# Extra matmuls of the identity on TensorE in the first twelve pairs of an attention and feed-forward kernel

## The chip, the cores and the metric

The kernel runs on one core of a Trainium2 chip. A core has a matrix engine (TensorE, in the profile PE, with its weight loads as PEld), VectorE (DVE), ScalarE (ACT), GpSimd (POOL), and SyncE (SP), which here only issues DMAs. Each engine serves its own instructions in the order in which the program gives them, and engines wait for one another through semaphores. The metric is the time of one execution on the device in microseconds (us). The matrix engine accumulates in PSUM, which holds eight banks of 512 float32 columns on 128 partitions.

## The reference

```python
scores = (1 / sqrt(64)) * q @ k.T            # 8 batches, 12 heads, 448 x 64
m = max(scores, axis=-1)
e = exp(scores - m)
attn = e / (sum(e, axis=-1) + exp(-m) + 1e-09)
x = (attn @ v)                               # heads side by side: 3584 x 768
h = x @ w_in                                 # 768 x 2048
g = h * tanh(log(1 + exp(h)))
out = g @ w_out                              # 2048 x 768
```

All inputs and the output are float32; the kernel computes in bfloat16 with float32 accumulation.

## The kernel before

Work goes by pairs of heads: 48 pairs, six to a batch. A pair's scores are made in four steps. In pairs 0 to 11 each of the first three steps makes two blocks of 128 query rows, one of each head, from 64 rows of the transposed query and key (L255 and L258), and the fourth makes the two remaining blocks of 64 rows side by side (L263 and L266). From pair 12 on the two heads are laid out diagonally and one matmul of 128 rows makes both (L249).

PSUM is split into three score tiles of two banks each, taken in turn (`sc_tiles`), and two single banks (`mo_tiles`), which are handed out and given back through the deque `mo_free`. The fourth step of a pair uses only the first bank of its score tile.

A step runs so: `scores_ahead` lets TensorE write the scores of the step three ahead as soon as a score tile is free; VectorE reduces them to the negated row maximum (L270); `exps` lets ScalarE take the exponentials, which give the row sums too (L283), and that frees the tile. After a pair VectorE makes the denominators (L296, L300) and scales the exponentials (`normalise`, L317; in some pairs on GpSimd, L315). The result is turned by a transposing DMA (L321) or, for pairs 5, 6 and 7, by TensorE in `turn_on_pe` (L332, seven transposes into one single bank, copied out by VectorE, L336). `av_pair` multiplies with the values (L358), and the copy into `xT` (L367) follows in `flush_late`, which runs at the start of the next step. Queries and keys are loaded by SyncE (L121), cast on GpSimd (L162 to L164), transposed by TensorE (L179) and copied out (`evac_qk`).

The order of all this is written out by hand. The head of the program takes pairs 0 to 5, step by step. Then units of three pairs follow, twelve steps each; in the first two of them (pairs 6 to 8, and 9 to 11) the turns and the value products of earlier pairs are placed at given steps (`TURN_AT`, `AV_AT`). After the twelve steps of a unit TensorE makes eight column blocks of the first feed-forward product (`mm1_mish`, L382, with the Mish function on ScalarE, L388), between which the next pairs' transposes and first scores stand. From pair 12 on matmuls of the second feed-forward product (L446) are filled into the steps. Weights are loaded by GpSimd's queue in pieces at given steps (`load_w`, L148).

Of the kernel before, what the change touches and what calls it, by code (L numbers as in the profile page):

```python
# [19 lines left out]
def kernel(  # L20
# [9 lines left out]
    nc = tc.nc  # L30
# [18 lines left out]
    STEPS = 4  # L49
# [3 lines left out]
    def pool(name, bufs, space=None):  # L53
# [18 lines left out]
    sc_tiles = [  # L72
        psum.tile([128, 2, 512], FP32, tag=f"sc{i}", name=f"sc{i}") for i in range(3)
    ]
    mo_tiles = [psum.tile([128, 512], FP32, tag=f"mo{i}", name=f"mo{i}") for i in range(2)]
    mo_free = deque(mo_tiles)

    ident = singles.tile([128, 128], BF16)
# [24 lines left out]
    def flush_late():  # L103
        while late:
            late.popleft()()
# [8 lines left out]
    def load_pair(p):  # L114
        if p >= N_PAIRS:
            return
        b, h0 = p // HP, (p % HP) * 2
        tiles = []
        for nm, src in (("q", q), ("k", k), ("v", v)):
            t = ld_pool.tile([SP_, 2, NT * D], FP32, tag=f"{nm}_f", name=f"{nm}_f")  # L120
            nc.sync.dma_start(  # L121
                out=t, in_=src[b, h0 : h0 + 2].rearrange("h (p t) d -> p h (t d)", t=NT)
            )
            tiles.append(t)
        loaded[p] = tiles
# [19 lines left out]
    def load_w(n):  # L145
        for _ in range(min(n, len(pieces))):
            dst, src = pieces.popleft()
            nc.gpsimd.dma_start(out=dst, in_=src.rearrange("(a p) c -> p a c", p=128))  # L148
# [38 lines left out]
    def evac_qk(p, act=False):  # L187
        if p >= N_PAIRS:
            return
        (q_ps, k_ps), own = qkT[p]  # L190
        mo_free.extend(own)
        qd = q_diag[p % 3]
        kT = qk_pool.tile([128, S], BF16, tag="kT", name="kT")
        if p < DIAG_FROM:
            qT = qd.rearrange("d i h r -> d (i h r)")[:, 0:S]
            qkT[p] = (qT, kT)
            if act:
                nc.scalar.mul(qT, q_ps[:, 0:S], SCALE)
            else:
                nc.vector.tensor_scalar(  # L200
                    out=qT, in0=q_ps[:, 0:S], scalar1=SCALE, scalar2=None, op0=ALU.mult
                )
        else:
            qkT[p] = (qd, kT)
            if p < DIAG_FROM + 3:
                nc.vector.memset(qd[0:64, :, 1, :], 0.0)
                nc.vector.memset(qd[64:128, :, 0, :], 0.0)
            for h in range(2):
                rows = slice(64 * h, 64 * h + 64)
                nc.vector.tensor_scalar(  # L210
                    out=qd[rows, :, h, :],
                    in0=q_ps[rows, 0:S].rearrange("d (i r) -> d i r", i=QB),
                    scalar1=SCALE, scalar2=None, op0=ALU.mult,
                )
        if p == 0 or own and not act:
            nc.vector.tensor_copy(out=kT, in_=k_ps[:, 0:S])
        else:
            nc.scalar.copy(kT, k_ps[:, 0:S])  # L218

    rg = dict(next=0, used=0)  # L220

    def scores_ahead(limit):

        while rg["next"] < limit and rg["used"] < len(sc_tiles):
            rg["used"] += 1
            scores(rg["next"])
            rg["next"] += 1
# [67 lines left out]
    def denominators(st):  # L295
        nc.vector.scalar_tensor_tensor(  # L296
            out=st["den"], in0=st["sums"], scalar=1e-9, in1=st["expm"],
            op0=ALU.add, op1=ALU.add,
        )
        nc.vector.reciprocal(out=st["rden"], in_=st["den"])  # L300
# [158 lines left out]
    first_mm2 = 2 * UNITS_PER_B  # L459
# [23 lines left out]

    weight = [5.2] + [1.0] * (steps - STEPS) + [0.4] * (STEPS - 1)

    LEAD = UNIT_PAIRS + 1
    LOAD_AT = (0, 3, 6)
    HEAD = HP
# [9 lines left out]
    W_AT = ({5: 1, 9: 1}, {1: 1, 4: 1, 5: 1, 7: 1, 9: 1, 11: 1}, {3: 1, 5: 1, 7: 1, 9: 1})  # L498
    for p in range(UNIT_PAIRS):
        load_pair(p)  # L500
    for p in range(2):
        cast_pair(p)
        transpose_pair(p)
        if p == 0:
            evac_qk(p, act=True)
            scores_ahead(3)
    load_pair(3)
    cast_pair(2)


    for p in range(HEAD):
        for s in range(STEPS):
            if s == 1 and p == 0:
                transpose_pair(p + 2)
            exps(p * STEPS + s)
            if p == 0 and s == 0:
                evac_qk(1, act=True)
            if s == 1:
                evac_qk(p + 2, act=True)
            if s:  # L520
                flush_late()
            scores_ahead(HEAD * STEPS + 3)
            if s == (2 if p == HEAD - 1 else 0):
                load_pair(p + 4)
            if s == 0:
                cast_pair(p + 3)
                load_w(1)
                if p:
                    denominators(att[p - 1])
            if s == 1:  # L530
                if p:
                    normalise(p - 1)
            if s == 3 and p + 3 < HEAD + 2:
                transpose_pair(p + 3)
            if s == 3 and p >= 3:
                av_pair(p - 3, act=True)
# [3 lines left out]
    for u in range(UNITS_PER_B, N_UNITS + 2 * UNITS_PER_B):  # L540
        attn = u < N_UNITS
        filler = deque()
        for part in plan.get(u, []):
            filler.extend(mm2_part(*part))
        total, done, acc = sum(w for _, w in filler), 0, 0.0
        p0 = u * UNIT_PAIRS
        if attn and u >= first_mm2:
            av_with.update({p0 + i: p0 + i - UNIT_PAIRS for i in range(UNIT_PAIRS)})
        end = min((u + 1) * UNIT_PAIRS, N_PAIRS) * STEPS

        for n in range(steps):
            pi, s = divmod(n, STEPS)
            p, idx = p0 + pi, p0 * STEPS + n
            late_tp = u == UNITS_PER_B and n == STEPS
            if late_tp:
                transpose_pair(p0 + 2)
            exps(idx)
            if late_tp:
                evac_qk(p0 + 2)
            if u == UNITS_PER_B + 1:  # L560
                for part in TURN_AT[1].get(n, []):
                    turn_on_pe(*part)
            flush_late()
            acc += weight[n]
            want = int(total * acc / sum(weight) + 1e-6)
            while done < want:
                fn, w = filler.popleft()
                fn()
                done += w
            scores_ahead(end)  # L570
            if n in LOAD_AT:
                load_pair(p0 + LOAD_AT.index(n) + LEAD)
                cast_pair(p0 + LOAD_AT.index(n) + LEAD - 1)
            if u - UNITS_PER_B < len(AV_AT):
                early = AV_AT[u - UNITS_PER_B]
                if n in early:
                    av_pair(early[n])
                if u == UNITS_PER_B:
                    for part in TURN_AT[0].get(n, []):
                        turn_on_pe(*part)  # L580
            elif s == (2 if pi else 0) and N_PAIRS <= p < N_PAIRS + UNIT_PAIRS:
                av_pair(p - UNIT_PAIRS)
            if u - UNITS_PER_B < len(W_AT):
                load_w(W_AT[u - UNITS_PER_B].get(n, 0))
        assert done == total

        moe = u < N_UNITS + UNITS_PER_B
        b, w = (u - UNITS_PER_B) // UNITS_PER_B, u % UNITS_PER_B
        nxt = p0 + UNIT_PAIRS
        todo = sorted(range(p0, nxt), key=lambda p: p in BY_PE)  # L590
        for f in range(FF_U):
            if moe:
                mm1_mish(b, w * FF_U + f)
            if u == UNITS_PER_B and f in (2, 6):
                load_w(1)
            if not attn:
                continue
            if f == 0:
                denominators(att[p0]["whole"])
                normalise(todo[0], dma=todo[0] not in BY_PE)  # L600
            if f == 3:
                scores_ahead(min(nxt * STEPS + 1, N_PAIRS * STEPS))
            if f in (1, 3, 5):
                transpose_pair(nxt + f // 2, bank=f // 2 % 2)
                evac_qk(nxt + f // 2)
            if f >= FF_U - 2:
                scores_ahead(min(nxt * STEPS + f - FF_U + 4, N_PAIRS * STEPS))
            if f == 3:
                normalise(todo[1], dma=todo[1] not in BY_PE)
            if f == 4:  # L610
                normalise(todo[2], dma=todo[2] not in BY_PE, on_pool=True)
        if moe and w == UNITS_PER_B - 1:
            gather_mid(b)
# [32 lines left out]
```

## Time and profile before

| what | value |
|---|---|
| three runs | 487.44, 489.59, 489.74 us; median 489.59 |
| the profiled execution | 492.75 us, of which its span 491.0 |
| busy over the span: PE, DVE, ACT, POOL | 450.5, 351.3, 350.2, 161.5 us |
| PE busy in 12 to 24 us, and in 96 to 108 us | 6.57 and 11.92 of 12 us |
| score matmul of 64 rows and 448 columns (L255), median | 529 ns |
| score matmul of 128 rows and 448 columns (L249), median | 353 ns |

The span runs from the first to the last instruction of the program. A row of the timeline gives start, duration, engine, line, operation, the tile written and those read with their shapes, how many instructions are merged, and, in brackets, how long the engine had been idle and what ended the wait. The chain of waits follows the work that ended last back to the start. A window's row gives for each engine the busy time and the number of instructions in it, then the granted clock of TensorE, the share of the DMA engines and the data rate. Matmuls overlap in the pipeline, so seven of them last less than seven times one.

### The profile page before, as it was taken

The numbers are of one execution on the slowest core, as the hardware profiler recorded it, in microseconds if no ns is written. First come the engines' busy times: TensorE is split into PE (matmuls) and PEld (weight loads), VectorE is DVE, ScalarE is ACT, GpSimd is POOL, SyncE is SP. The second block draws the span as 40 slices with busy tenths as digits, with TensorE's granted clock in tenths as the row PEclk, the third lists the DMA queues.
The fourth block names the chain that finished last, engine by engine and source line by source line (L and its number), as shares of the span: only waits on it lengthen the run. The fifth ranks groups of instructions, "written<-read, shape, count | busy, mean of one in ns | idle before, by whom it ended". The sixth has DMA issues, their size and how long they took to land.

```text
span 491.0 us, 8804 instructions
## 1 busy us (share of the span) xinstructions
PE 450.5 (92%) x2992; PEld 248.5 (51%) x2992; DVE 351.3 (72%) x702; ACT 350.2 (71%) x906; POOL 161.5 (33%) x266
## 2 busy tenths in 40 slices
PE   3556898798989999999999999999999999999996
PEld 1222444454644555555655555555556565556563
DVE  4798987978868787878788786878797878420021
ACT  4889678878777887979796878888797979502300
POOL 3622257454412534253413323253425230300000
PEclk9999998999999999999999999999999999999999
DMA  8999999999999999999998979998999686780112
GB/s 212 183 205 228 236 207 221 228 177 236 175 225 263 195 220 188 241 186 267 148 248 187 223 164 210 211 213 227 176 265 179 167 176 140 132 159 21 45 37 93
DMA packets 209452, 92.19 MB, mean 188 GB/s; under 512 B 166272, under 2 KB 205952, under 8 KB 209408
## 3 DMA queue, kind: packets, MB, share of 16 engines
q1 hardware_dynamic: 201920, 85.35, 81.2%
q0 software_dynamic: 7488, 6.29, 8.8%
q8 instruction: 23, 0.38, 0.3%
q14 instruction: 21, 0.17, 0.1%
HBM read 45.61 MB, written 11.01 MB: 115 GB/s over the span
## 4 chain that ended last, share of the span: by engine, by line
PE 68%; DVE 14%; ACT 9%; DMA 4%; issue 2%; SPq 1%; POOL 0%; DVEq 0%; ACTq 0%
PE mo L446 24%; PE mo L382 23%; PE sc L249 8%; ACT en L283 8%; DVE negm L270 7%; PE sc L358 6%; DVE en L317 4%; PE sc L382 3%; PE sc L179 3%; DMA eT<-en 3%; DMA k_f<-in_k_dram 1%; PE mo L358 1%; PE sc L255 1%; DVE xT L367 1%; DVE eT L336 1%
## 5 line engine op out<-in xcount | busy, mean ns | idle before, releaser
L283 ACT ACTIVATE en<-sc,negm 128x448 bf16<-128x448 f32 x336 | 209.7, 637 | 28.7 <-DVE negm L270 16.3
L270 DVE TENSOR_REDUCE negm<-sc 128x2 f32<-128x896 f32 x192 | 182.4, 969 | 61.5 <-PE sc L249 48.7
L446 PE MATMUL mo<-w_out_sb,gT 128*128 128x384 bf16 (+1 forms) x896 | 142.1, 303 | 0.0
L382 PE MATMUL mo<-xT,w_in_sb 128*128 128x448 bf16 x672 | 140.2, 352 | 0.9 <-DVE xT L367 0.9
L388 ACT ACTIVATE gT<-mo 128x448 bf16<-128x448 f32 x112 | 59.4, 543 | 73.5 <-PE mo L382 73.3
L446 PEld LDWEIGHTS <-gT 128*128 128x128 bf16 x896 | 84.0, 98 | 46.8 <-issue 1.3
L382 PEld LDWEIGHTS <-w_in_sb 128*128 128x128 bf16 x768 | 72.8, 98 | 64.9 <-issue 4.2
L315 POOL TENSOR_SCALAR en<-en,rden 128x448 bf16<-128x448 bf16 x98 | 61.7, 649 | 115.8 <-DVE rden L308 106.0
L249 PE MATMUL sc<-kT,qd 128*128 128x448 bf16 x252 | 71.6, 354 | 1.8 <-DVE qd L210 1.5
L162 POOL CAST q_bf<-q_f 112x512 bf16<-112x512 f32 x47 | 29.1, 619 | 121.8 <-DMA q_f<-in_q_dram 105.4
L283 ACT ACTIVATION_READ_ACCUMULATOR en<-sc,negm 128x1 f32 x336 | 69.2, 206 | 0.0
L317 DVE TENSOR_SCALAR en<-en,rden 128x448 bf16<-128x448 bf16 x238 | 67.2, 354 | 0.9
L433 DVE COPY o_sb<-mo 128x384 f32<-128x384 f32 (+1 forms) x64 | 32.1, 502 | 41.3 <-PE mo L446 41.2
L249 PEld LDWEIGHTS <-qd 128*128 128x128 bf16 x252 | 24.0, 97 | 32.1 <-issue 13.9
L358 PE MATMUL sc<-eT,v_bf 112*64 112x448 bf16 x288 | 34.1, 357 | 4.1 <-ACT en L283 2.0
L164 POOL CAST v_bf<-v_f 112x512 bf16<-112x512 f32 x48 | 29.6, 618 | 20.6 <-DMA v_f<-in_v_dram 19.1
L358 PEld LDWEIGHTS <-v_bf 112*64 112x64 bf16 x384 | 21.1, 114 | 25.7 <-issue 16.9
L255 PE MATMUL sc<-kT,qd 64*128 64x448 bf16 x36 | 17.5, 508 | 17.4 <-ACT en L283 16.0
L163 POOL CAST k_bf<-k_f 112x512 bf16<-112x512 f32 x47 | 29.2, 622 | 6.7 <-DMA k_f<-in_k_dram 5.9
L210 DVE TENSOR_SCALAR qd<-sc 64x448 bf16<-64x448 bf16 x72 | 27.8, 386 | 0.9
L218 ACT COPY kT<-sc 128x448 bf16<-128x448 bf16 x39 | 20.8, 534 | 6.8 <-PE sc L179 6.8
L446 PE MATMUL mo<-w_out_sb,mid 128*128 128x384 bf16 x128 | 24.9, 326 | 0.0
(50 smaller groups left out, 306.9 us busy)
## 6 DMA issues: line engine op xcount, KB each, us to landing
q_f<-in_q_dram SPq DMA_DIRECT2D x48, 224.0 KB, 5.5
k_f<-in_k_dram SPq DMA_DIRECT2D x48, 224.0 KB, 5.6
v_f<-in_v_dram SPq DMA_DIRECT2D x48, 224.0 KB, 5.9
w_in_sb<-in_moe_w_in_dram POOLq DMA_DIRECT2D x12, 256.0 KB, 5.6
w_out_sb<-in_moe_w_out_dram POOLq DMA_DIRECT2D x8, 384.0 KB, 8.6
out_dram<-o_sb SPq DMA_DIRECT2D x7, 336.0 KB, 3.5
out_dram<-o_sb SPq DMA_DIRECT2D x8, 288.0 KB, 4.8
out_dram<-o_sb SPq DMA_DIRECT2D x8, 240.0 KB, 3.4
```

Of the source, the lines that this page charges most:

```text
L163: cast_k(out=k_bf, in_=k_f.rearrange(by_t, t=NT))
L164: nc.gpsimd.tensor_copy(out=v_bf, in_=v_f)
L249: nc.tensor.matmul(sc[:, bk, 0:S], lhsT=qT[:, i].rearrange("d h r -> d (h r)"), rhs=kT, start=True, stop=True,)
L270: nc.vector.tensor_reduce(out=negm, in_=sc[:, 0 : len(cols), 0:S], axis=AX.X, op=ALU.max, negate=True)
L283: nc.scalar.activation(out=st["en"][:, :, c, 0:SP_], in_=sc[:, bk, 0:S].rearrange("q (j c) -> q j c", j=NT), func=AF.Exp, bias=st["negm"][ ...
L315: nc.gpsimd.tensor_scalar(scalar2=1.0, op0=ALU.mult, op1=ALU.mult, **args)
L317: nc.vector.tensor_scalar(scalar2=None, op0=ALU.mult, **args)
L358: nc.tensor.matmul(av[h * 64 : (h + 1) * 64, 0:S], lhsT=v_bf[:, h, j * D : (j + 1) * D], rhs=e_h, start=(j == 0), stop=(j == NT - 1),)
L382: nc.tensor.matmul(h_ps[:, 0:S], lhsT=w_in_sb[:, dm, ff * 128 : (ff + 1) * 128], rhs=xT[b][:, dm, :], start=(dm == 0), stop=(dm == DM_T - 1),)
L388: nc.scalar.activation(out=gT[b][:, ff, :], in_=h_ps[:, 0:S], func=AF.Mish)
L433: nc.vector.tensor_copy(out=o_sb[:, cols], in_=st["o"][:, 0:n_cols])
L446: nc.tensor.matmul(st["o"][:, 0:n_cols], lhsT=src[:, ff, c0 : c0 + 128], rhs=w_out_sb[:, ff, cols], start=(ff == 0), stop=(ff == FF_T - 1),)
```

## The change

A helper `keep_busy(n, bank)` issues n matmuls of the 128 x 128 identity with itself into the first 128 columns of a PSUM bank. Each starts and ends an accumulation of its own, and nothing reads the result. It is called:

- 24 times into the second bank of the third score tile before the first pair's transposes, 6 times there after them, and 10 times into a free single bank after the first three scores;
- in the head, 8 times after the scores of each of a pair's first three steps: at the first step into the second bank of the score tile that was just written with the fourth scores (which fill only the first bank), at the other two into a free single bank;
- in the first two units after it, 8 times after the scores of each pair's first step into that second bank, and at the other steps into a single bank if both single banks are free.

That makes 40, 144 and twice 96 matmuls, 376 in all, each with a weight load of the identity.

```diff
+    def keep_busy(n, bank):
+        for _ in range(n):
+            nc.tensor.matmul(bank[:, 0:128], lhsT=ident, rhs=ident, start=True, stop=True)
...
+    BUSY = 8
...
     for p in range(UNIT_PAIRS):
         load_pair(p)
+    keep_busy(24, sc_tiles[2][:, 1, :])
     for p in range(2):
         cast_pair(p)
         transpose_pair(p)
         if p == 0:
             evac_qk(p, act=True)
+            keep_busy(6, sc_tiles[2][:, 1, :])
             scores_ahead(3)
+            keep_busy(10, mo_free[0])
...
             scores_ahead(HEAD * STEPS + 3)
+            if s == 0:
+                keep_busy(BUSY, sc_tiles[(p * STEPS + 3) % 3][:, 1, :])
+            elif s < 3:
+                keep_busy(BUSY, mo_free[0])
...
             scores_ahead(end)
+            if u < first_mm2 and s == 0:
+                keep_busy(BUSY, sc_tiles[(idx + 3) % 3][:, 1, :])
+            elif u < first_mm2 and len(mo_free) == 2:
+                keep_busy(BUSY, mo_free[0])
```

## The prediction

> **What bounds the kernel now.** I read the page's slices and chain first, then busy times of short windows, then the timeline of one pair of heads and of one later unit.
>
> ```profile
> PE   3556898798989999999999999999999999999996
> DVE  4798987978868787878788786878797878420021
> PEclk9999998999999999999999999999999999999999
> PE 68%; DVE 14%; ACT 9%; DMA 4%; issue 2%; SPq 1%; POOL 0%; DVEq 0%; ACTq 0%
> ```
>
> From about slice 9 (105 us) TensorE is busy without a break and carries the chain. Before that it idles, and the chain runs through VectorE's reduces and ScalarE's exponentials. So the end moves by whatever the first 100 us gain or lose. The dummies lie in just that stretch.
>
> The clock row reads full speed in the first 65 us, but the matmuls do not: scores from 64 rows (L255) take 529 ns up to there, and 128-row scores of the same 448 columns (L249, later) 353. Windows of 3.4 us show what the speed follows:
>
> ```profile
> 61.79:65.20 3.41, 3.41 (x20) 1.02 (x20) 3.31 (x5) 2.63 (x9) 1.27 (x3) 1.00 1.07 263
> 65.20:68.61 3.41, 3.41 (x29) 1.88 (x26) 2.66 (x5) 3.38 (x9) 2.88 (x5) 1.00 1.13 257
> 78.85:82.27 3.42, 1.03 (x12) 0.76 (x10) 2.14 (x5) 3.41 (x10) 3.41 (x7) 1.00 1.13 273
> 82.27:85.68 3.41, 3.40 (x21) 1.99 (x21) 3.17 (x5) 3.24 (x11) 2.27 (x5) 0.51 1.05 229
> 89.09:92.51 3.42, 2.00 (x22) 1.01 (x21) 3.42 (x5) 2.08 (x7) 2.48 (x4) 1.00 1.22 232
> ```
>
> Columns: window, length, PE busy, PEld, DVE, ACT, POOL, granted clock, DMA share, GB/s. After the fully busy 61.79 to 65.20 the array is fast (L358 falls from 581 to 353 ns). After 78.85 to 82.27, busy for 1.03 of 3.42, it is slow again, and here the clock row says 0.51. With 2.00 busy it stayed fast. The 1.00 of the first 65 us is therefore no record of speed.
>
> [...]
>
> One pair of the head (timeline):
>
> ```profile
> 22.32 0.58 PE L263 MATMUL sc<-kT,qd 64*64 64x448 bf16 x1
> 22.62 2.60 DVE L270 TENSOR_REDUCE negm<-sc 128x2 f32<-128x896 f32 x3
> ...
> 25.13 0.53 PE L255 MATMUL sc<-kT,qd 64*128 64x448 bf16 x1 [2.23 <-ACT en L283]
> ...
> 25.79 1.09 DVE L270 TENSOR_REDUCE negm<-sc 128x2 f32<-128x896 f32 x1 [0.26 <-PE sc L258]
> ...
> 45.48 0.62 DVE L270 TENSOR_REDUCE negm<-sc 128x1 f32<-128x448 f32 x1 [1.90 <-PE sc L266]
> ```
>
> The pair's last scores are written at 22.32; their reduce is the third of the three, ending about 25.2. TensorE's next scores start at 25.13, and VectorE has only 0.26 us of slack for them.
>
> The first unit after the head, VectorE, then TensorE, then the same transposes once fast:
>
> ```profile
> 51.58 1.92 DVE L317 TENSOR_SCALAR en<-en,rden 128x448 bf16<-128x448 bf16 x7
> 53.42 1.61 DVE L270 TENSOR_REDUCE negm<-sc 128x1 f32<-128x448 f32 x2
> 55.49 1.07 DVE L270 TENSOR_REDUCE negm<-sc 128x2 f32<-128x896 f32 x1
> 64.99 0.61 DVE L270 TENSOR_REDUCE negm<-sc 128x1 f32<-128x448 f32 x1
> ```
> ```profile
> 49.47 0.58 PE L263 MATMUL sc<-kT,qd 64*64 64x448 bf16 x1
> 51.53 0.53 PE L255 MATMUL sc<-kT,qd 64*128 64x448 bf16 x1 [1.48 <-ACT en L283]
> 54.33 0.99 PE L332 MATMUL mo<-ident,en 128*112 128x128 bf16 x7
> 65.89 1.31 PE L382 MATMUL mo<-xT,w_in_sb 128*128 128x448 bf16 x6
> ```
> ```profile
> 86.48 0.60 PE L332 MATMUL mo<-ident,en 128*112 128x128 bf16 x7
> ```
>
> **What is added.** 376 matmuls of 128 columns with their weight loads: 40 ahead, 144 in the head (three groups of 8 per pair), 96 in each of the next two units. Nothing else moves on any queue. The group after a pair's last scores writes the free bank of the tile just written. In the built program its first matmul waits for VectorE's reduce of that same tile, and the exponential of that tile waits for the group. So it does not fill the idle time ahead of that reduce: it starts when the idle time is over, and the next real scores stand behind it. That TensorE is served in order the trace shows at 57.98: L263 needed exponentials done at 56.3 and stood behind transposes that waited until 57.14.
>
> **Price of a group.** No such matmul is in the trace; nearest are the seven L332, also 128 columns with a load each. Slow: 0.99 less the last one's 0.31, over six gaps, 0.113 each, 0.9 for 8. Fast: 0.60 less 0.22, 0.063 each, 0.5 for 8. Both ends stay.
>
> **The 40 ahead and the first pair.** They lie before data land (q at 3.52, casts of POOL until 12.17): 0 to 0.2, I take 0.
>
> **Head, pairs 2 to 6.** The group starts at 25.2 and ends at 25.7 (fast) or 26.1 (slow), so scores start 0.6 to 1.0 later than 25.13; fast scores give 0.18 back: 0.45 to 1.0 a pair. Four pairs: 1.8 to 4.0. VectorE's idle 1.90 at 45.48, when transposes and slow L358 keep TensorE, swallows up to 1.9 of it. The sixth pair, where scores 45.30 must now wait for a reduce ending near 46.1, adds 0.7 to 1.2. Head: 0.7 to 3.3; I take 2.0, as waits of some 2 us between groups leave the array slow in some pairs. The group after the next scores lies in the 1.54 us that TensorE waits for exponentials before 27.23: 0. The one after that delays scores from 27.85 to 28.6, but their reduce starts only at 29.6, behind the normalise: 0. Without these covers each would cost 0.5 to 0.9 a pair. ScalarE's new wait, the pair's fourth exponential at 27.04 for a group done by 26.1, costs nothing either; behind it stand only the next pair's exponentials.
>
> **Unit at 49 to 66** (pairs 7 to 9; its times before the shift). The scores of 49.47 are reduced only at 53.42, behind the normalise; their group starts at 54.0 where scores had started at 51.53. After 4 us of idling the array is slow: group 0.9, scores 0.55, next reduce 55.5 for 53.97, +1.5. Then three steps: TensorE needs 0.4 scores, 0.9 group, 0.8 transposes, 2.1 a step, where reduces came every 1.53 (55.49, 57.02); with the pair's own transposes in the third this is +2.3, and a full window has made the array fast near 60. The second pair's group: end of reduce to next reduce is 0.5 in the trace (59.83 to 60.33), now 0.5 group, 0.45 transposes, 0.4 scores, 0.5 copy, +1.3, here +5.1 in all; fast L358 return 0.3, so the last reduce is at +4.8. The tail: from that reduce's end 65.6 to the first matmul by w_in took 0.3; now 8, 16, and 8 dummies (2.0) and fast L358 (0.75) stand there, with hand-overs 2.9, +2.6. It starts at +7.4; TensorE's 0.56 wait at 71.56 swallows part: +6.8.
>
> **Unit at 81 to 94** (pairs 10 to 12). The same plan. Reduce at 82.93: scores wait for 82.15, 0.9 and transposes, +1.7; three steps +1.2; second pair's group +1.3; small waits +0.2; so last reduce +4.4. The tail of 32 dummies, against an idle 0.65 at 93.84, +3.0: +7.4.
>
> Sum: 2.0 + 6.8 + 7.4 = 16.2. If every group costs 0.5, no step is longer than VectorE's, and 0.7 in the head, then 1.1 (first group) + 1.3 + 2.0 (tail less the wait) = 4.4, and 1.2 + 1.3 + 3.0 = 5.5 are left, 10.6 in all. If every one costs 0.9: 3.3 in the head, and in each unit 0.4 for each of its other groups more with L358 slow, some 11 and 12: 26. After 105 us TensorE is the bound, so nothing returns it. The profiled execution took 492.75 (span 491.0), and becomes 509; it stands 3.2 above the median 489.59 of the runs shown, so I forecast 505.8.
>
> [...]
>
> **Rivals.**
> Faster: the groups fit into waits and the array is fast from the first pair. On the chain before 95 us slow pieces are six L255 (0.18 each), two L358 blocks (1.65 to 0.95), transposes (about 1): 3.5 in all, 486. It decides if the groups wait for nothing later than the exponentials the next scores wait for. Against it: the reduce ends at 25.2 against scores at 25.13, at 53.97 against 51.53.
> Half returned: the transpose DMA of 125.13 took 12.44 us, the median 6.4; a later, emptier queue could give back 6.0: +10, 499.5. Against it: the loads and w_out pieces beside it are issued by the same steps and move along.
> The change doesn't do what it says: waits keep each pair below a busy window, the array stays slow, groups cost 0.9: +26, 515. Against it: with groups queued TensorE runs 5 us on end in a pair, 7 in the units.
> No change: gain 3.5 against waits hidden to 3.5, 489.6.
>
> **How the numbers follow.** Forecast 0.72 (own range 500 to 511, from +10.6 to +21); half returned 0.10; stays slow 0.08; faster 0.06; no change 0.04. 505.8 is the likeliest. Range 497 to 512: it holds the first and second, and leaves out 515 and the last two. A measurement of this kernel tells about 0.5% (2.4 us) from no change. Faster 0.06, same 0.04, slower 0.90.
>
> **What would show it.** In the changed profile: the added line on TensorE (L225), its groups after a pair's last scores released by the reduce; next scores 0.5 to 1 us after that reduce in the head; the 32 dummies between the last reduce and the first matmul by w_in; first matmul by w_in near 75 and the second unit's near 110; 64-row scores at 350 ns in part. Wrong if the w_in matmuls start where they did, or if the groups end before the exponentials do.

## The result, and the profile after

The changed kernel takes 506.32 us (median of four runs, 504.81 to 509.3), the kernel before on the same chip 489.22 (487.44 to 489.74). The ratio is 1.0352, with a 95% interval of 1.0316 to 1.0389: 17.1 us slower. The forecast was 505.8, its range 497 to 512.

The profiled execution of the changed kernel took 506.91, span 505.0. The one of before that the prediction read (492.75) was 3 us longer than that kernel's usual run, so shifts below are taken against a second profiled execution of it, of 489.64 with a span of 487.9.

From the page of the changed kernel, the slices of TensorE, VectorE and the granted clock, and the engines' shares of the chain:

```profile
PE   7596788899899999999999999999999999999996
DVE  4888776667868878787868777978788887530021
PEclk9958599799999999999999999999999999999999
PE 73%; DVE 12%; ACT 6%; DMA 5%; issue 3%; SPq 0%; DVEq 0%; ACTq 0%
```

TensorE's busy time rose by 20 us over the whole span, from 449.9 to 469.9, but of the first ten slices (counted from 0) it is fuller in four (0, 2, 7 and 9) and emptier in two (4 and 5). Its share of the chain rose from 68% to 73% and ScalarE's fell from 9% to 6%; the second profile of before has 71% and 7%, so over half of that is the spread of executions. VectorE, which had the chain there, is emptier in slices 4 to 9. Idle time was filled, and the engine that set the pace was slowed.

The matmuls of the identity, and what TensorE was waiting for before them (view of one line; us and times):

```profile
L225 PE MATMUL sc<-ident x126: 216/219/314, 1.4 to 105.6; 128*128 128x128 bf16 x126
...
  DVE negm L275: 17.6, 12
...
  ACT en L288: 3.4, 4
```

There are twelve pairs, and in each TensorE stood idle ahead of the group behind the last scores, until the reduce of the tile whose free bank the group writes: 17.6 us in all. This is the wait that the prediction read out of the built program. Its sum is not the loss, near as the two are: in before TensorE idled 16.0 us ahead of L255 for ScalarE's exponentials, so most of this idle time was there already. What costs is that it now ends later. The last line shown is the opposite wait, of ScalarE's exponentials for a group: four times, 3.4 us in all. None of the four lies on the chain that ended last.

A pair of the head and the end of the sixth pair, timeline of the changed kernel (all lines of code are five further down: L275 is the reduce, L260 the 64-row scores, L363 the value products, L387 the product by `w_in`):

```profile
21.71 2.61 DVE L275 TENSOR_REDUCE negm<-sc 128x2 f32<-128x896 f32 x3
24.37 1.01 PE L225 MATMUL sc<-ident 128*128 128x128 bf16 x8 [2.43 <-DVE negm L275]
...
46.25 0.61 PE L225 MATMUL sc<-ident 128*128 128x128 bf16 x8 [2.59 <-DVE negm L275]
...
47.26 1.09 DVE L275 TENSOR_REDUCE negm<-sc 128x2 f32<-128x896 f32 x1 [0.76 <-PE sc L263]
```

The group starts 0.05 us after the last of the three reduces (21.71 + 2.61), with TensorE idle for 2.43 before it. At 46.25 the next reduce is seen to pay: VectorE idles 0.76 us for scores that had to stand behind the group.

The first unit, VectorE and TensorE together:

```profile
55.98 1.01 PE L225 MATMUL sc<-ident 128*128 128x128 bf16 x8 [3.20 <-DVE negm L275]
...
57.59 1.09 DVE L275 TENSOR_REDUCE negm<-sc 128x2 f32<-128x896 f32 x1 [1.66 <-PE sc L263]
...
70.75 0.61 DVE L275 TENSOR_REDUCE negm<-sc 128x1 f32<-128x448 f32 x1
71.42 0.61 PE L225 MATMUL sc<-ident 128*128 128x128 bf16 x8 [0.94 <-DVE negm L275]
71.86 1.06 PE L225 MATMUL mo<-ident 128*128 128x128 bf16 x16
72.85 0.95 PE L363 MATMUL mo<-eT,v_bf 112*64 112x448 bf16 x8
73.73 0.62 PE L225 MATMUL mo<-ident 128*128 128x128 bf16 x8
```

Both terms of the forecast are here. At 55.98 the group ends 3.20 us of idle time that it was meant to fill, and VectorE then waits 1.66. From the last reduce's end, 71.36, to the first matmul by `w_in` at 74.19 there are 2.83 us, of which the 32 dummies take most. In the first profile of before that stretch was 0.3.

The shift of the changed kernel against the second profile of before, at reduces (counted from 0, four steps a pair) and at each unit's first matmul by `w_in`:

| point | shift, us | by this stretch | forecast |
|---|---|---|---|
| first reduce of the first unit (27) | +2.5 | head +2.5 | +2.0 |
| reduce 28, behind the first group | +4.2 | +1.7 | +1.5 |
| reduce 31, after three steps | +5.5 | +1.3 | +2.3 |
| reduce 32, behind the second pair's group | +6.7 | +1.2 | +1.3 |
| last reduce of the unit (35) | +6.3 | -0.4 | -0.3 |
| first matmul by `w_in` (74.19) | +9.2 | +2.9 | +2.6 |
| first reduce of the second unit (36) | +9.2 | 0 | -0.6 |
| reduce 40 | +11.2 | +2.0 | +1.7 |
| reduces 43 and 44 | +12.2, +13.4 | +1.0, +1.2 | +1.2, +1.3 |
| last reduce (47) | +13.6 | +0.2 | +0.2 |
| first matmul by `w_in` (108.93) | +16.8 | +3.2 | +3.0 |
| end | +17.1 | +0.3 | 0 |

### The profile page after: what moved, and what is told of

Read it like the earlier page. It is cut to its first block, busy times and chain, and to the rows that moved or that the text cites. A ratio compares the mean times of both kernels' runs of the same rounds, so it can differ in the third digit from the quotient of the medians.

```text
span 505.0 us, 9566 instructions
## 1 busy us (share of the span) xinstructions
PE 469.9 (93%) x3368; PEld 273.0 (54%) x3368; DVE 350.2 (69%) x702; ACT 350.3 (69%) x906; POOL 160.7 (32%) x266
## 4 chain that ended last, share of the span: by engine, by line
PE 73%; DVE 12%; ACT 6%; DMA 5%; issue 3%; SPq 0%; DVEq 0%; ACTq 0%
PE mo L387 23%; PE mo L451 22%; PE sc L254 8%; DVE negm L275 7%; PE sc L363 6%; ACT en L288 5%; DMA eT<-en 4%; DVE en L322 3%; PE sc L387 3%; PE sc L179 3%; PE mo L225 2%; PE sc L225 2%; PE sc L260 1%; PE mo L363 1%; DVE xT L372 1%
## 5 line engine op out<-in xcount | busy, mean ns | idle before, releaser
L275 DVE TENSOR_REDUCE negm<-sc 128x2 f32<-128x896 f32 x192 | 182.5, 970 | 66.0 <-PE sc L254 48.9
L387 PE MATMUL mo<-xT,w_in_sb 128*128 128x448 bf16 x672 | 140.2, 352 | 0.3 <-DVE xT L372 0.3
L387 PEld LDWEIGHTS <-w_in_sb 128*128 128x128 bf16 x768 | 72.8, 98 | 63.6 <-issue 2.9
L320 POOL TENSOR_SCALAR en<-en,rden 128x448 bf16<-128x448 bf16 x98 | 61.4, 646 | 135.3 <-DVE rden L313 107.7
L322 DVE TENSOR_SCALAR en<-en,rden 128x448 bf16<-128x448 bf16 x238 | 65.9, 349 | 0.9
L225 PEld LDWEIGHTS <-ident 128*128 128x128 bf16 x376 | 28.1, 115 | 30.0 <-issue 28.6
L363 PE MATMUL sc<-eT,v_bf 112*64 112x448 bf16 x288 | 34.1, 357 | 3.4 <-ACT en L288 2.0
L164 POOL CAST v_bf<-v_f 112x512 bf16<-112x512 f32 x48 | 29.5, 615 | 15.7 <-DMA v_f<-in_v_dram 14.1
L363 PEld LDWEIGHTS <-v_bf 112*64 112x64 bf16 x384 | 20.2, 110 | 22.7 <-issue 13.6
L225 PE MATMUL sc<-ident 128*128 128x128 bf16 x126 | 12.5, 263 | 19.0 <-DVE negm L275 17.6
```

The source lines that it names most:

```text
L164: nc.gpsimd.tensor_copy(out=v_bf, in_=v_f)
L225: nc.tensor.matmul(bank[:, 0:128], lhsT=ident, rhs=ident, start=True, stop=True)
L275: nc.vector.tensor_reduce(out=negm, in_=sc[:, 0 : len(cols), 0:S], axis=AX.X, op=ALU.max, negate=True)
L320: nc.gpsimd.tensor_scalar(scalar2=1.0, op0=ALU.mult, op1=ALU.mult, **args)
L322: nc.vector.tensor_scalar(scalar2=None, op0=ALU.mult, **args)
L363: nc.tensor.matmul(av[h * 64 : (h + 1) * 64, 0:S], lhsT=v_bf[:, h, j * D : (j + 1) * D], rhs=e_h, start=(j == 0), stop=(j == NT - 1),)
```

## The experiments

Three theories were set against one another. **In line**: the loss is the wait for the reduce and, beside it, TensorE's time for the dummies that stand ahead of real work. **Waits alone**: the matmuls themselves cost nothing, only the new wait does. **Clock**: the added matmuls make the array slower, whatever they wait for. All these kernels compute the full result.

**One matmul in place of each eight.** It leaves every wait and takes away seven eighths of TensorE's work in the groups.

```diff
-    BUSY = 8
+    BUSY = 1
```

> The changed kernel with one dummy in place of eight in every group of the head and the units (46 + 40 of them at the start stay 24, 6 and 10); every wait stays where it is. In line (the groups cost what TensorE spends on them behind the reduce and ahead of the w_in matmuls, plus the wait): the waits stay, 0.5 to 0.9 us shrinks to about 0.1 per group; head +0.4, first unit +2.7, second +3.4, in all +6 over before (4 to 9). Waits alone (the array time of the dummies is hidden, only the wait for the reduce costs): as the changed kernel, +14 to +17. Clock (the extra matmuls lower the granted clock, 0.966 against 0.997, and that costs): almost nothing left, 0 to +2.

Measured: 499.63, ratio 1.0212 (1.0189 to 1.0235), 10.5 us slower than before. That lies between the two forecasts, and both missed. The second unit's end shows why (timeline):

```profile
98.60 0.27 PE L225 MATMUL sc<-ident 128*128 128x128 bf16 x1 [1.35 <-DVE negm L275]
98.80 1.70 PE L363 MATMUL mo<-eT,v_bf 112*64 112x448 bf16 x8
...
100.75 1.70 PE L363 MATMUL mo<-eT,v_bf 112*64 112x448 bf16 x8
```

The value products take 1.70 us a block, the slow array's time; in the changed kernel they took 0.95. The granted clock reads 0.50 here from 83.52 to 104.00 us, in the changed kernel's second unit only from 88.59 to 95.42. The waits remain, and the seven further matmuls that kept TensorE busy behind each are gone. So a wait here has two costs: the time that the next scores start late, and an array that falls slow in the pause. I had priced the first only. The second costs 0.75 for each of the two blocks shown, and as much for one at 92.69.

Up to the first unit's end the sizes were right: +0.6 in the head and +2.9 in the unit, for +0.4 and +2.7 expected, with the array fast from 59.6 us on. The second unit lost 6.8 for 3.4 expected. Why the array stayed slow there for so long is in part open, since one window was filled and changed nothing (columns as in the prediction):

```profile
93.76:97.17 3.41, 3.41 (x19) 1.34 (x15) 2.43 (x4) 1.46 (x5) 0.00 (x0) 0.50 1.31 203
97.17:100.58 3.41, 2.06 (x13) 0.77 (x11) 1.41 (x3) 3.39 (x12) 0.00 (x0) 0.50 0.62 96
```

That the array is slow here with fewer dummies than in the changed kernel, where it is fast in most of the same stretch, also speaks against the clock theory.

**The group ahead of the fourth scores.** The same 376 matmuls into the same banks, but the group of each pair is issued before the scores that share its tile, so that it waits only for what these scores wait for. In the head:

```diff
+            if s == 0:
+                keep_busy(BUSY, sc_tiles[(p * STEPS + 3) % 3][:, 1, :])
             scores_ahead(HEAD * STEPS + 3)
-            if s == 0:
-                keep_busy(BUSY, sc_tiles[(p * STEPS + 3) % 3][:, 1, :])
-            elif s < 3:
+            if 0 < s < 3:
                 keep_busy(BUSY, mo_free[0])
```

and the same in the units.

> The changed kernel with the group at a pair's first step issued ahead of the fourth scores instead of behind them (same bank, same number of dummies), in the head and in both units; it then waits only for the exponentials and the reduce of the tile's earlier use, which those scores wait for anyway. In line: the wait for the new reduce is gone, so the head costs 0 to -1, each unit keeps its steps and its tail of 24 dummies, some +3.5 each; in all +6 (4 to 9). Waits alone: 0 to +1. Clock: the same number of matmuls, so +14 to +17 stay.

Measured: 495.05, ratio 1.012 (1.0091 to 1.0149), 6.0 us slower than before and 11 less than the changed kernel. A pair of it (timeline):

```profile
48.10 0.61 PE L225 MATMUL sc<-ident 128*128 128x128 bf16 x8 [0.34 <-ACT en L288]
48.64 0.37 PE L268 MATMUL sc<-kT,qd 64*64 64x448 bf16 x1
```

The group now waits for ScalarE's exponential, as the scores do, and VectorE's reduce no longer releases any L225. In-line time remains: the groups still stand ahead of scores and, at the ends of the units, ahead of the `w_in` matmuls, whose shifts are +1.6 and +4.7. From a unit's last reduce to these matmuls, where 24 dummies stand, the shift grows by 1.6 and 1.8. The clock theory falls: as many dummies as in the changed kernel cost a third of its loss. Waits alone falls too, for it gave at most 1 here.

**Head alone, units alone.** One kernel keeps the 40 ahead and the head's groups, the other only those of the two units.

```diff
-            if u < first_mm2 and s == 0:
-                keep_busy(BUSY, sc_tiles[(idx + 3) % 3][:, 1, :])
-            elif u < first_mm2 and len(mo_free) == 2:
-                keep_busy(BUSY, mo_free[0])
```

> The changed kernel without the 192 dummies of the two units; the 40 ahead and the 144 of the head stay as they are. In line and waits alone: the head's share, +2 (1 to 4); 64-row scores in the head at 350 to 360 ns. Clock: about half of the loss for half of the dummies, +7 to +9.

> The changed kernel without the 40 dummies ahead and the 144 of the head; the 192 of the units stay. In line: what the units cost, +12 (10 to 14), with the first w_in matmuls of the first unit about 6.5 later than before and those of the second about 13 later. Waits alone: the same. Clock: about half, +7 to +9. Together with the head-only run it tells whether the shares add up to the whole change.

Measured: the head alone 490.71, ratio 1.0035 (1.0015 to 1.0056), +1.6; the units alone 501.15, ratio 1.0233 (1.0209 to 1.0256), +12. Both agree with the in-line sizes, and the 64-row scores of the head alone took 360 ns in the median. With the units alone the first matmuls by `w_in` came 5.5 and 12.0 us late, each 1 less than expected. Together the two losses make 13.6 and not 17.1. With the head alone the delay is 3.2 us at the head's end but 2.1 at the first matmul by `w_in`: the unit has some slack for a late start. In the whole change no slack shows: the +9.2 at the first unit's end is still +9.2 at the second's first reduce. That TensorE, with groups in most steps, sets the pace there is my reading of it; the chain of waits fits, which has TensorE alone from 71.42 to 85.44 us, but no run tested it by itself.

**Before, once more.**

> The kernel before itself, for a second profiled execution of it. The first took 492.75 us, 3 to 4 above the median of its runs; if that is only the spread of executions, this one lies at 488 to 490.5 and its reduces in the head some 1 us earlier than in the first profile, as the units-only run's were. Any theory.

Measured: 489.64, span 487.9, and from the second to the sixth pair (reduces 4 to 22) its reduces stand 0.9 to 1.4 us earlier than in the first profile, as expected. It is the profile that the shifts above are read against.

**The gain that was hoped for, without its price.** The head's groups ahead of the scores, no groups in the units: the order in which the "faster" rival could come true, if anywhere.

> The changed kernel with the head's first group of each pair issued ahead of the fourth scores, and without the 192 dummies of the units. In line: the groups now lie in TensorE's waits for exponentials, the array is fast in most of the head, the value products that held back a reduce for 1.9 us shrink, and nothing waits longer: -1.5 (-3 to 0) against before. If the units' slow stretches and not the head set the end: 0. Waits of another kind left in the head (the group ahead of the scores delays them): +1 to +2.

Measured: 490.41, ratio 1.0021 (1.0005 to 1.0037), 1.15 us slower; a gain of 1.5 had been expected. The chain of waits at the end of its head (start, duration, what):

```profile
40.17 0.61 POOL q_bf L162
...
40.78 0.62 POOL k_bf L163
...
42.00 1.63 PE mo L363 x4
43.63 0.97 PE sc L225 x8
44.60 0.51 PE sc L268
```

The head's end comes from GpSimd's casts of a loaded query and key. That load was issued 1.66 us earlier than in before (33.65 against 35.31) but landed only 0.65 earlier (40.01 against 40.66), so the faster start brought little forward. And where the array has fallen slow all the same (0.97 for a group, 1.63 for value products) the group stands in the chain between the value products and the scores: the reduces ahead of it (20 to 22) stand at -0.5, the one behind it (23) at +0.3. The first unit gains nothing either: the reduces of its first nine steps stand at +0.4.

**Without the last groups of each unit.** No groups into the single banks from a unit's tenth step on, 24 matmuls less in each unit:

```diff
-            elif u < first_mm2 and len(mo_free) == 2:
+            elif u < first_mm2 and n < 9 and len(mo_free) == 2:
```

> The changed kernel without the 24 dummies of each unit that stand between the unit's last scores' group and the first w_in matmul (steps 10 to 12); the group of 8 before them stays. In line: 24 at 0.063 us, 1.5 per unit, come back, -3 against the changed kernel, so +14 over before (13 to 15.5); the w_in matmuls of the first unit start 1.5 earlier than in the changed kernel. If a later wait (xT's copy, the denominators) takes their place: 0 to -1.

Measured: 503.36, ratio 1.0281 (1.025 to 1.0313): 14.1 above before, 3.0 less than the changed kernel's median. Forty-eight matmuls that wait for nothing new cost 3.0 us, 0.0625 each. The runs of the two kernels overlap (501.26 to 505.45, and 504.81 to 509.3), so that figure alone is loose; the traces agree with it. From a unit's last reduce to the first matmul by `w_in` the shift grows by 1.5 and 1.7 here, by 2.9 and 3.2 in the changed kernel: 1.4 and 1.5 less for 24 dummies each. A dummy ahead of the `w_in` matmuls cost just its own time here, 0.058 to 0.063 us. The first of these matmuls came at 74.52 all the same, and not 1.5 earlier than the changed kernel's 74.19 as expected, because the head of this execution ended 1.5 later.

**The 40 ahead alone.**

> The kernel before with only the 40 dummies ahead of and around the first pair. In line: 0 (-0.5 to +0.5), as the first scores wait for the loads and casts. Fast array from the start: -1, if the first pairs' scores run at 350 ns because of it.

Measured: 489.38, ratio 1.0011 (0.9987 to 1.0035): no difference. The array was fast for the first pair's scores, for which a gain of 1 us had been held possible:

```profile
6.05 0.35 PE L260 MATMUL sc<-kT,qd 64*128 64x448 bf16 x1
```

So the fast array alone gained nothing there. The clock row of this kernel has more to say, and is shown in the last section.

## Why the prediction was right

**The wait for the reduce.** It was the step on which everything stood, and the rows at 24.37, 55.98 and 71.42 show it as forecast. With it in place the loss is 17.1, without it 6.0.

**The price of a group.** Taken from L332 at 0.5 fast and 0.9 slow. Eight L225 measured 0.61 to 0.62 fast and 1.01 to 1.04 slow as shown, each less what runs into the next instruction. By the slopes, 16 fast in 1.06 less the last one's 0.22 over 15 gaps is 0.056 each, and 24 slow in 2.74 (the 24 ahead of all work) less 0.31 over 23 is 0.106, so 0.45 and 0.85 a group. The nearest rows were 7 to 12% high.

**The head.** +2.5 against 2.0, within 0.7 to 3.3 here; the same head measured +3.2 and +4.0 in the profiles of two other kernels, so the term scatters and its upper end was too low. Its course was as described: +3.5 at the sixth pair's reduce 21, back to +0.7 at 23 where VectorE had been idle, and up again to +2.7 behind the last group.

**The units.** +6.7 and +7.6 (16.8 less 9.2) against 6.8 and 7.4. The first agrees by errors that cancel: three steps with groups cost 1.3 where I had 2.3, and the 0.56 us of waiting that was to swallow part of the tail swallowed nothing, while group and tail were each 0.2 to 0.3 dearer. The second unit agrees term by term. The tail is the best-proved term: 2.9 and 3.2 us measured, and the kernel without 48 of the 64 matmuls gives 3.0 back, 1.4 and 1.5 of it seen in the trace.

**When the array turns fast.** "Near 60" in the first unit. Windows of the changed kernel, cut where its granted clock changes (columns as in the prediction):

```profile
57.87:61.28 3.41, 3.41 (x30) 2.81 (x27) 2.47 (x3) 1.70 (x5) 0.64 (x2) 0.50 0.78 229
61.28:64.70 3.42, 2.05 (x29) 1.55 (x28) 3.26 (x6) 2.32 (x8) 2.19 (x4) 1.00 1.06 269
...
92.00:95.42 3.42, 3.42 (x29) 2.67 (x28) 2.88 (x4) 1.34 (x4) 3.42 (x7) 0.50 0.94 146
95.42:98.83 3.41, 2.18 (x30) 1.66 (x29) 2.99 (x5) 2.57 (x8) 2.03 (x3) 1.00 1.03 142
```

Behind the unit's first fully busy window, with the dummies in it, the clock is 1.00 from 61.28, where in the first profile of before the array turned fast at 65.20. So there the change does what it says, about one window earlier, and the 0.4 us that the table shows regained between reduces 32 and 35 stand against 9.2 lost. In the second unit the clock is 1.00 from 95.42; less the 9.2 of shift that is 86.2, where before had it from 85.68, so there it is no earlier. It had also been slow for longer, from 88.59, two windows where before had one. In the head the array was fast from 10.08 to 23.74 and from 37.39 to 47.63 and slow between and behind, as the groups at 24.37 (1.01 us) and 46.25 (0.61 us) show; the head still lost. These rows agree with what the prediction read out of before's windows, that the array is fast behind a fully busy one; that reading alone would have given a gain, 3.5 us by the first rival, and the time went up by 17.1. Nor does it hold everywhere: the window at 93.76 above, with one dummy in each place, was busy for 3.41 of 3.41 us and the array stayed slow.

**The rivals.** *Faster* falls with the group-ahead kernels: without the new wait the change still loses 6.0, and in the head alone 1.15. I had made its price 3.5 of gain, and no run's time shows any of it; the largest advance of a reduce in any profile is 0.6 us, and it passes within a step. *Half returned*: after 108.93 the shift stays between 16.5 and 17.1 to the end, and the longest transposing DMA near there takes 11.7 us to land for 12.4 before; it moved along. The reason given for the stretch behind 105 us, TensorE busy without a break, is not quite so: from 108 to 120 us before had it busy for 10.0 of 12, and from 109.8 to 118.8 the chain runs through VectorE and ScalarE. The whole stretch moved along all the same. *Stays slow*: refuted for the whole by the windows, though it came true for stretches of the head, and for 20.5 us around the second unit of the kernel with one dummy in each place. *No change* holds for the 40 ahead alone.

**What was missed** lay behind the prediction, in two expectations: the waits with one dummy each (+6 expected, +10.5 measured), as I left out that a wait can also leave the array slow; and the head with its groups first (a gain of 1.5 expected, a loss of 1.15 measured), as I counted a faster array as gain in a stretch that loads and VectorE bound. The sizes of wait and work in the whole change can't be parted exactly: with one dummy each it loses 10.5, and the further seven add 6.6, but those seven also make the array faster (the two blocks of value products at the second unit's end took 0.95 us each with them, 1.70 without).

## What to carry to other kernels

TensorE took its instructions in order here: it waited 2.43 us for the group at 24.37, and the next scores came only behind that group, at 25.32. The idle time of such an engine can only be filled for nothing by work that waits for no more than the next real instruction waits for; look up what the filler's destination is tied to, since here a free bank counted as part of the tile whose other bank was still being read (twelve waits for the reduce, 17.6 us). Behind that, ask whose wait ends last: when another engine or a load sets the pace, a faster TensorE was worth next to nothing here (489.38 us with the 40 ahead, 490.41 with the head's groups first, 489.26 before), and each filler matmul ahead of the `w_in` products, on TensorE's own path, cost its full time (0.0625 us by the runs). Test the order first (filler ahead of or behind the real instruction): here that alone moved 11 us.

## What the runs showed of the hardware

A granted clock of 1.00 did not always stand for a fast array. Before's row reads 9 in slices 0 to 5, while its 64-row scores took 529 ns, the slow array's time, and stays at 9 where the array turned fast, at 65.20. With only the 40 dummies ahead, which changed no time (489.38 us against 489.26), the row of the granted clock is

```profile
PEclk9555599999989999999999999999999999999999
```

with 5 in slices 1 to 4. Its matmuls go with that: the first scores at 6.05 us took 0.35 us, those at 12.68, when the recorded clock had fallen to 0.50, 0.55. So the row reads 1.00 for a slow array in the one run and 0.50 in the other; why, no run shows. The mean granted clock of a run was therefore no measure of how fast its array was: 0.997 in the first profile of before, 0.943 with the 40 ahead, for the same time (492.75 and 492.61 us). Nor did it rank kernels: the one with one dummy each has 0.933 and is 7 us faster than the changed one with 0.966.

In the traces of before and of the changed kernel the changes of the granted clock lie whole multiples of 3.41 us apart (in before 17.07 us from the turn at 65.20 to the fall, and 3.41 from there; 13.65, 13.65, 10.24, 13.65, 27.31 and 6.83 in the changed kernel), but the two runs have different starts for them: 61.28 in the changed kernel and 65.20 in before are some 4 us apart. In the two unit windows shown of the changed kernel, busy for 3.41 or 3.42 us, the array became fast, and so it did in before's 61.79 to 65.20. That is not all there is to it: at 93.76 in the kernel with one dummy each a window busy for 3.41 us left the array slow, and in the one with the 40 ahead TensorE was busy for nine tenths or more of slice 4 (49.1 to 61.4 us) at a mean granted clock of 0.5 to 0.6. A window of 3.06 (at 26.38, groups ahead of the scores) was enough, one of 3.13 (at 86.93, one dummy each) was not. A fast array stayed fast in before with 2.00 of 3.42, and was slow again after 1.03. So busy time as the profile shows it does not settle when the clock changes, and no run here tells what does.
